# A fused recurrence and feed-forward kernel: w_in's first columns in two transfers, ScalarE copies two pairs' turned q, a new order table

## The chip, the cores and the metric

The kernel runs on one core of a Trainium2 chip. The metric is device time in microseconds (us). The engines of the core are TensorE (PE in the profile; PEld is its loading of weights), VectorE (DVE), ScalarE (ACT), GpSimd (POOL) and SyncE (SP). Each takes its instructions in program order. Loads, stores and the transposing transfers are issued by SP, the weights' transfers by POOL.

## The reference

Two stages in a row, all in float32. First a gated linear recurrence for 4 batches of 8 heads over 768 steps with heads of 48 elements, then a feed-forward layer (384 to 2048 to 384) with a leaky ReLU.

```python
f = 1.0 / (1.0 + np.exp(-f_logit))
for t in range(S):                                  # S = 768
    state = f[:, :, t, :, None] * state + np.einsum('bhd,bhe->bhde', k[:, :, t], v[:, :, t])
    y[:, :, t] = np.einsum('bhd,bhde->bhe', q[:, :, t], state)
x = y.transpose(0, 2, 1, 3).reshape(B * S, H * D)   # 3072 x 384
h = x @ w_in                                        # 384 x 2048
out = np.maximum(0.01 * h, h) @ w_out               # 2048 x 384
```

## The kernel before

The 768 steps are cut into 6 chunks of 128, and the 4 batches into 2 halves of two. A chunk with a half is a pair j (12 of them, j = 0 to 11), and each of its two batches is a unit a (0 or 1). A word such as `mx_0_1` in the order table means the part `mx` of pair 0, unit 1.

For a unit the work goes as follows. SP loads f, k, q and v (`Lf`, `Lk`, `Lq`, `Lv`, line 99). ACT forms the logarithm of the gate (`gate`, lines 135 and 136), PE sums it along the chunk with a triangle of ones and once more to the chunk's end (`cs`, lines 141 and 144), and ACT takes three exponentials of it (`dec`, lines 151, 152 and 155). DVE or POOL scales k and q by them (`k`, line 160; `q`, line 166), and POOL casts v (`v`, lines 173 and 174). PE turns k and q into PSUM (`tk`, `tq`, line 187), and DVE copies the turned tiles out (`ck`, `cq`, line 190); from pair 6 on a transposing transfer of SP does this instead (`xk`, `xq`, line 193). PE forms the scores (`sc`, line 206), DVE multiplies them by the triangle (`mk`, line 211), and PE mixes them with v, and with the state of the chunks before (`mx`, line 239). DVE copies the result out as the feed-forward input xT (`xt`, line 245). Beside that PE forms the chunk's own state (`pt`, line 250), DVE adds it (`sf`, lines 255 and 256) and POOL decays it (`sb`, lines 260 and 263).

The feed-forward layer takes w_in in groups. For pairs 0 to 3, whose units are done one by one, `uu_j_a_g` is group g of 4 blocks of 128 hidden columns (12 matmuls, line 290) and `pu` its leaky ReLU on ACT (line 295). Later pairs do both units at once (`up`, line 277; `pr`, line 283). `dn_j_a_q` is a quarter of the down-projection of a unit (4 matmuls, line 300); the last unit goes in two column parts (`dp`, line 322). DVE copies the result (`ob`, line 305) and SP stores it (`st`, line 313).

The weights come by POOL's transfers, which cast them from float32 to bfloat16: `W_0` to `W_2` bring the columns 0 to 511, 512 to 1023 and 1024 to 2047 of w_in (line 111), `W_3` to `W_6` the four quarters of w_out's rows (line 115). A one-element POOL copy (line 108) makes the first of them wait for v of pair 1, unit 0. `H_4` (line 127) is a small transfer on SP that waits for `W_4`; the loads of pair 2 stand behind it.

Nothing is scheduled by the compiler: `manual_schedule` keeps the order in which the words of the table (lines 348 to 403) are carried out, and each engine takes its own share of them in that order. PSUM tiles rotate: `ps_g` has 4 buffers for `cs`, `tp`, `pw`, `py` and `pt` (a score takes two), so each waits for the reader of the fourth one before it; `ps_m` has 2 for `uu` and `up`, `ps_o` 2 for `dn`. The loads rotate through 6 buffers of each kind.

Of the kernel before, what the change touches and what calls it, by code (L numbers as in the profile page):

```python
# [15 lines left out]
def kernel(  # L16
# [87 lines left out]
    def weights(piece, x, j, a):  # L104

        if (x, j, a) not in seen:
            seen.add((x, j, a))
            nc.gpsimd.tensor_copy(out=gate_w[:, 0:1], in_=raw(j, "fkqv"[x])[0:1, a, H - 1, D - 1:D])
        if piece < len(w_in_cols):
            lo, hi = w_in_cols[piece]  # L110
            nc.gpsimd.dma_start(out=w_in_b[piece], in_=moe_w_in[:, lo:hi].rearrange("(k p) n -> p k n", p=128))  # L111
        else:
            n = NF // 4
            part = piece - len(w_in_cols)
            nc.gpsimd.dma_start(  # L115
                out=w_out_b[:, part * n:(part + 1) * n, :],
                in_=moe_w_out[part * n * 128:(part + 1) * n * 128, :].rearrange("(p a) n -> p a n", a=n))
# [167 lines left out]
    def up_unit(j, a, g):  # L285
        pm = st[j]["pu", a, g] = ps_m.tile([128, 4, 128], FP32, name="pm", tag="pm")
        for i in range(4):
            ff = 4 * g + i
            for kk in range(NK):
                nc.tensor.matmul(pm[:, i, :], w_in(kk, ff), st[j]["xT"][:, kk, a, :],  # L290
                                 start=(kk == 0), stop=(kk == NK - 1))

# [66 lines left out]
    uu_1_1_3 dec_2_0 v_2_0 Lf_3_0 ob_0_0 dn_1_0_0 pu_1_1_2 dn_1_1_0 q_2_0 st_0_0 gate_2_1 dn_1_0_1 k_2_0 st_0_1 tq_2_0
    tk_2_0 cq_2_0 dn_1_1_1 Lk_3_0 ck_2_0 cs_2_1 sc_2_0 Lq_3_0 dec_2_1 v_2_1 pt_2_0 mk_2_0_0 dn_1_0_2 Lv_3_0 sb_0_1  # L360
    mk_2_0_1 dn_1_1_2 pu_1_1_3 q_2_1 gate_3_0 dn_1_0_3 Lf_3_1 sf_2_0 mx_2_0 Lk_3_1 dn_1_1_3 xt_2_0 tq_2_1 k_2_1 Lq_3_1
    uu_2_0_0 ob_1_0 cs_3_0 pu_2_0_0 Lv_3_1 uu_2_0_1 cq_2_1 dec_3_0 tk_2_1 v_3_0 uu_2_0_2 st_1_0 ck_2_1 pt_2_1 pu_2_0_1
    q_3_0 dn_2_0_0 Lf_4_0 sf_2_1 pu_2_0_2 uu_2_0_3 sb_1_1 k_3_0 Lk_4_0 sc_2_1 pu_2_0_3 tq_3_0 mk_2_1_0 Lq_4_0 dn_2_0_1
    gate_3_1 mk_2_1_1 tk_3_0 dn_2_0_2 Lv_4_0 v_3_1 cq_3_0 cs_3_1 ck_3_0 mx_2_1 Lf_4_1 dec_3_1 ob_1_1 sc_3_0 xt_2_1
    dn_2_0_3 st_1_1 k_3_1 q_3_1 pt_3_0 uu_2_1_0 mk_3_0_1 Lk_4_1 sb_2_0 tk_3_1 mk_3_0_0 pu_2_1_0 uu_2_1_1 Lq_4_1 sf_3_0
    dn_2_1_0 pu_2_1_1 Lv_4_1 mx_3_0 v_4_0 gate_4_0 pt_3_1 xt_3_0 tq_3_1 Lf_5_0 uu_2_1_2 gate_4_1 sf_3_1 dn_2_1_1
    Lk_5_0 ck_3_1 pu_2_1_2 uu_2_1_3 cq_3_1 ob_2_0 Lq_5_0 sc_3_1 pu_2_1_3 cs_4_0 mk_3_1_1 dn_2_1_2 dec_4_0 st_2_0
    mk_3_1_0 cs_4_1 dn_2_1_3 Lv_5_0 dec_4_1 k_4_0 q_4_0 mx_3_1 uu_3_0_0 Lf_5_1 v_4_1 gate_5_0 k_4_1 tk_4_0 Lk_5_1
    tq_4_0 xt_3_1 q_4_1 uu_3_0_1 pu_3_0_0 ck_4_0 tk_4_1 Lq_5_1 sb_2_1 cq_4_0 pu_3_0_1 cs_5_0 uu_3_0_2 ck_4_1 dec_5_0
    Lv_5_1 pt_4_0 sb_3_0 uu_3_1_0 sf_4_0 pu_3_0_2 Lf_6_0 tq_4_1 pt_4_1 k_5_0 dn_3_0_0 pu_3_1_0 v_5_0 sf_4_1 Lk_6_0  # L370
    gate_5_1 uu_3_1_1 sb_3_1 cq_4_1 dn_3_0_1 Lq_6_0 ob_2_1 pu_3_1_1 sc_4_2 q_5_0 uu_3_1_2 st_2_1 mk_4_0_0 dn_3_0_2
    mk_4_0_1 v_5_1 pu_3_1_2 Lv_6_0 tq_5_0 mk_4_1_0 uu_3_1_3 Lf_6_1 mk_4_1_1 tk_5_0 uu_3_0_3 Lk_6_1 ck_5_0 mx_4_2
    cq_5_0 pu_3_0_3 Lq_6_1 cs_5_1 xt_4_0 sb_4_0 dn_3_1_0 dec_5_1 Lv_6_1 xt_4_1 dn_3_0_3 sb_4_1 Lf_7_0 pu_3_1_3 pt_5_0
    dn_3_1_1 ob_3_0 sf_5_0 gate_6_0 up_4_0 st_3_0 q_5_1 k_5_1 dn_3_1_2 Lk_7_0 tq_5_1 dn_3_1_3 pr_4_0 cq_5_1 Lq_7_0
    cs_6_0 ob_3_1 tk_5_1 dec_6_0 up_4_1 Lv_7_0 ck_5_1 v_6_0 pt_5_1 cs_6_1 pr_4_1 sf_5_1 up_4_2 st_3_1 dec_6_1 dn_4_0_0
    Lf_7_1 up_4_3 pr_4_2 k_6_0 sc_5_2 Lk_7_1 pr_4_3 up_4_4 mk_5_0_0 Lq_7_1 dn_4_0_1 q_6_0 mk_5_1_0 pr_4_4 xk_6 pt_6_0
    mk_5_0_1 up_4_5 mk_5_1_1 pt_6_1 pr_4_5 up_4_6 xq_6 sf_6_0 mx_5_2 gate_7_0 sf_6_1 Lv_7_1 up_4_7 xt_5_0 sb_5_0
    dn_4_0_2 Lf_8_0 xt_5_1 pr_4_6 cs_7_0 pr_4_7 up_5_0 dec_7_0 Lk_8_0 cs_7_1 dn_4_0_3 pr_5_0 up_5_1 Lq_8_0 ob_4_0
    dec_7_1 dn_4_1_0 st_4_0 up_5_2 pr_5_1 q_7_0 sc_6_2 Lv_8_0 pr_5_2 dn_4_1_1 mk_6_0_0 Lf_8_1 up_5_3 sb_5_1 mk_6_1_1
    xq_7 dn_4_1_2 mk_6_1_0 pr_5_3 k_7_0 up_5_4 mk_6_0_1 Lk_8_1 dn_4_1_3 pr_5_4 Lq_8_1 mx_6_2 v_7_0 up_5_5 xt_6_0 xk_7  # L380
    sb_6_0 pt_7_0 xt_6_1 gate_8_0 dn_5_0_0 sf_7_0 up_6_0 Lv_8_1 sb_6_1 ob_4_1 dn_5_0_1 Lf_9_0 pr_5_5 cs_8_0 pr_6_0
    up_6_1 dec_8_0 cs_8_1 st_4_1 up_6_2 pr_6_1 dn_5_0_2 Lk_9_0 pr_6_2 pt_7_1 up_6_3 sf_7_1 Lq_9_0 dec_8_1 dn_6_0_0
    Lv_9_0 v_8_0 up_5_6 pr_6_3 sc_7_2 Lf_9_1 pr_5_6 k_8_0 up_6_4 mk_7_0_0 Lk_9_1 up_5_7 mk_7_1_0 pr_6_4 dn_6_0_1
    mk_7_0_1 Lq_9_1 q_8_0 pr_5_7 up_6_5 mk_7_1_1 xk_8 dn_5_0_3 pr_6_5 mx_7_2 ob_5_0 xq_8 dn_6_0_2 gate_9_0 xt_7_0
    sb_7_0 up_6_6 st_5_0 xt_7_1 pt_8_0 sb_7_1 up_7_0 sf_8_0 Lv_9_1 pr_6_6 pt_8_1 cs_9_0 pr_7_0 sf_8_1 up_7_1 dec_9_0
    Lf_10_0 up_6_7 cs_9_1 Lk_10_0 pr_7_1 dn_5_1_0 pr_6_7 up_7_2 Lq_10_0 dec_9_1 dn_6_0_3 Lv_10_0 up_7_3 pr_7_2 ob_6_0
    sc_8_2 v_9_0 Lf_10_1 pr_7_3 up_7_4 mk_8_1_1 st_6_0 dn_6_1_0 k_9_0 mk_8_0_1 pr_7_4 up_7_5 mk_8_0_0 Lk_10_1 dn_6_1_1
    mk_8_1_0 pr_7_5 q_9_0 xk_9 up_7_6 mx_8_2 pr_7_6 Lq_10_1 up_7_7 xq_9 xt_8_0 sb_8_0 dn_6_1_2 xt_8_1 pr_7_7 dn_5_1_1
    gate_10_0 Lv_10_1 dn_6_1_3 Lf_11_0 up_8_0 dn_5_1_2 pr_8_0 cs_10_0 Lk_11_0 up_8_1 dn_5_1_3 pr_8_1 Lq_11_0 cs_10_1
    dec_10_0 up_8_2 ob_5_1 Lv_11_0 pt_9_0 dn_8_0_0 dec_10_1 sf_9_0 st_5_1 up_8_3 ob_6_1 pr_8_2 k_10_0 sc_9_2 pr_8_3  # L390
    st_6_1 up_8_4 mk_9_0_0 dn_8_0_1 Lf_11_1 mk_9_1_0 sb_8_1 pr_8_4 up_8_5 xk_10 mk_9_1_1 pt_9_1 mk_9_0_1 dn_7_0_0
    pr_8_5 Lk_11_1 sf_9_1 up_8_6 Lq_11_1 mx_9_2 pr_8_6 dn_8_0_2 xt_9_0 sb_9_0 Lv_11_1 up_8_7 xt_9_1 dn_7_0_1 q_10_0
    pr_8_7 up_9_0 gate_11_0 dn_7_0_2 v_10_0 xq_10 dn_8_0_3 pr_9_0 dn_7_0_3 ob_8_0 sb_9_1 cs_11_0 up_9_1 st_8_0 ob_7_0
# [43 lines left out]
```

## Time and profile before

| what | us |
|---|---|
| median of 3 runs | 184.77 (184.28 to 184.93) |
| the profiled execution's own time | 185.62 |
| its span, first to last instruction | 183.9 |
| busy: PE, PEld, DVE, ACT, POOL | 169.2, 133.1, 90.0, 99.1, 75.2 |
| down-projection matmuls (line 300), 368 of them | 71.6 |
| up-projection matmuls (lines 277 and 290), 384 each | 51.5 and 27.5 |

Times in the trace count from the span's start. Busy time is the time in which at least one instruction of the engine ran; matmuls overlap, so a mean duration is longer than the distance from one to the next. The table of slices gives the busy share of each fortieth of the span (4.6 us) in tenths. The chain of waits is followed back from the last instruction: each row is a start, a length, an engine and a line, with the number of instructions merged. A DMA queue's row gives packets, megabytes and the time that the packets took as a share of 16 engines' time; q0 is POOL's queue, q1 is SP's.

### The profile page before, as it was taken

The numbers are of one execution on the slowest core, as the hardware profiler recorded it, in microseconds if no ns is written. First come the engines' busy times: TensorE is split into PE (matmuls) and PEld (weight loads), VectorE is DVE, ScalarE is ACT, GpSimd is POOL, SyncE is SP. The second block draws the span as 40 slices with busy tenths as digits, with TensorE's granted clock in tenths as the row PEclk, the third lists the DMA queues.
The fourth block names the chain that finished last, engine by engine and source line by source line (L and its number), as shares of the span: only waits on it lengthen the run. The fifth ranks groups of instructions, "written<-read, shape, count | busy, mean of one in ns | idle before, by whom it ended". The sixth has DMA issues, their size and how long they took to land.

```text
span 183.9 us, 5443 instructions
## 1 busy us (share of the span) xinstructions
PE 169.2 (92%) x2264; PEld 133.1 (72%) x2264; DVE 90.0 (49%) x188; ACT 99.1 (54%) x201; POOL 75.2 (41%) x138
## 2 busy tenths in 40 slices
PE   0467699999999999999999999999999999999993
...
GB/s 117 199 202 181 189 205 215 190 179 225 209 207 184 196 208 193 210 211 224 151 224 174 218 169 177 226 233 136 237 211 150 77 100 46 0 53 36 43 86 86
DMA packets 118208, 30.23 MB, mean 164 GB/s; under 512 B 113064, under 2 KB 117288, under 8 KB 118184
## 3 DMA queue, kind: packets, MB, share of 16 engines
...
## 4 chain that ended last, share of the span: by engine, by line
PE 87%; POOL 4%; SPq 3%; DMA 2%; issue 2%; DVE 0%; POOLq 0%
PE po L300 33%; PE pm L277 24%; PE pm L290 13%; PE py L239 5%; PE pw L206 4%; SPq L99 3%; DMA v_raw<-in_v_dram 2%; PE pt L250 2%; PE tp L187 2%; PE cs L141 2%; PE po L322 1%; POOL w_in_b L111 1%; POOL w_out_b L115 1%; PE cs L144 1%; POOL v_b L173 1%
## 5 line engine op out<-in xcount | busy, mean ns | idle before, releaser
L300 PE MATMUL po<-w_out_b,gT 128*128 128x384 bf16 x368 | 71.6, 326 | 0.0
L283 ACT ACTIVATE gT<-pm 128x512 bf16<-128x512 f32 x64 | 38.1, 599 | 32.5 <-PE pm L277 32.0
L277 PE MATMUL pm<-xT,w_in_b 128*128 128x256 bf16 x384 | 51.5, 273 | 0.0
L300 PEld LDWEIGHTS <-gT 128*128 128x128 bf16 x368 | 34.0, 98 | 15.8 <-issue 0.2
L277 PEld LDWEIGHTS <-w_in_b 128*128 128x128 bf16 x384 | 40.8, 114 | 5.3
L305 DVE COPY osb<-po 128x384 f32<-128x384 f32 x23 | 12.7, 555 | 47.4 <-PE po L300 47.2
L211 DVE TENSOR_TENSOR wm<-pw,ut 128x512 bf16<-128x512 f32 x48 | 30.2, 683 | 10.9 <-PE pw L206 10.7
L295 ACT ACTIVATE gT<-pm 128x512 bf16<-128x512 f32 x32 | 19.1, 600 | 22.7 <-PE pm L290 22.1
L290 PE MATMUL pm<-xT,w_in_b 128*128 128x128 bf16 x384 | 27.5, 226 | 0.0
L173 POOL CAST v_b<-v_raw 128x384 bf16<-128x384 f32 (+1 forms) x18 | 12.1, 672 | 35.5 <-DMA v_raw<-in_v_dram 25.1
L290 PEld LDWEIGHTS <-w_in_b 128*128 128x128 bf16 x384 | 24.7, 116 | 1.7 <-issue 0.2
L166 POOL TENSOR_TENSOR qh<-q_raw,a_t 128x384 bf16<-128x384 f32 (+1 forms) x12 | 15.7, 1309 | 14.6 <-ACT a_end L155 8.9
L245 DVE CAST xT<-py 128x384 bf16<-128x384 f32 x24 | 12.6, 552 | 12.0 <-PE py L239 11.8
L263 POOL CAST sb<-sf 64x192 bf16<-64x192 f32 x40 | 14.3, 357 | 9.5 <-PE py L239 7.3
L151 ACT ACTIVATE em_t<-cs 128x384 bf16<-128x384 f32 x24 | 11.8, 494 | 9.8 <-PE cs L144 8.9
L141 PE MATMUL cs<-lf,ut 128*128 128x384 bf16 x24 | 8.5, 352 | 6.9 <-ACT lf L136 6.1
L135 ACT ACTIVATE e_t<-f_raw 128x384 f32<-128x384 f32 (+1 forms) x18 | 11.4, 632 | 5.8 <-DMA f_raw<-in_f_logit_dram 5.8
L160 POOL TENSOR_TENSOR kh<-k_raw,em_t 128x768 bf16<-128x768 f32 x6 | 9.9, 1646 | 8.1 <-ACT em_t L151 8.0
L152 ACT ACTIVATE a_t<-cs 128x384 bf16<-128x384 f32 x24 | 11.9, 494 | 0.0
L136 ACT ACTIVATE lf<-e_t 128x384 bf16<-128x384 f32 (+1 forms) x18 | 11.4, 631 | 0.6
L255 DVE TENSOR_TENSOR sf<-sf,pt 64x192 f32<-64x192 f32 x20 | 6.9, 343 | 9.6 <-PE pt L250 4.3
L260 POOL TENSOR_TENSOR sf<-sf,a_end 128x192 f32<-128x192 f32 x20 | 10.6, 529 | 0.6 <-DVE sf L256 0.2
...
## 6 DMA issues: line engine op xcount, KB each, us to landing
...
```

The lines of the kernel that those rows point to most:

```text
L141: nc.tensor.matmul(t[:, 0:H * D], ut, lf[:, a, :, 0:D], start=True, stop=True)
L166: eng.tensor_mul(qhs[j % NR][:, a, :, 0:D], raw(j, "q")[:, a], st[j]["a"][:, a].rearrange("t a (h d) -> t a h d", d=D))
L173: nc.gpsimd.tensor_copy(out=vb[:, a], in_=raw(j, "v")[:, a])
L211: nc.vector.tensor_mul(wm, st[j].pop(("pw", a, i)), ut[:, None, :].to_broadcast([128, P2, 128]))
L245: nc.vector.tensor_copy(out=xT[:, :, a, :], in_=st[j].pop(("py", a))[:, 0:NK, :])
L263: nc.gpsimd.tensor_copy(out=sb[rows, a, :, i * D:i * D + D], in_=sf[rows, a])
L277: nc.tensor.matmul(pm[:, i, :], w_in(kk, ff), st[j]["xT"][:, kk].rearrange("t a s -> t (a s)"), start=(kk == 0), stop=(kk == NK - 1))
L283: nc.scalar.activation(gT[:, 2 * g:2 * g + 2, :], st[j].pop(("pm", g)), AF.Prelu, alpha=0.01)
L290: nc.tensor.matmul(pm[:, i, :], w_in(kk, ff), st[j]["xT"][:, kk, a, :], start=(kk == 0), stop=(kk == NK - 1))
L295: nc.scalar.activation(gT[:, 4 * g:4 * g + 4, 128 * a:128 * a + 128], st[j].pop(("pu", a, g)), AF.Prelu, alpha=0.01)
L300: nc.tensor.matmul(po, st[j]["g"][:, ff, 128 * a:128 * a + 128], w_out_b[:, ff, :], start=(ff == 0), stop=(ff == NF - 1))
L305: nc.vector.tensor_copy(out=osb, in_=st[j].pop(("po", a)))
```

## The change

The first 512 columns of w_in come as two transfers of 256 (`W_0`, `W_1`), so the other pieces' numbers go up by one, and the hold, `H_5`, waits for the same quarter of w_out as before. Hidden columns 0 to 511 are dealt to blocks in two sets of 256 instead of one of 512, and the rows of w_out's first quarter are laid out to match, in 256 rows of two instead of 128 of four. The first group of pair 0's two units is computed in halves of 6 matmuls (`uh`) with a leaky ReLU each (`ph`). For pairs 0 and 1 ACT copies the turned q. A transposing transfer may take one unit (no word of the table uses that). The whole order table is new; its beginning is shown, up to the first `cs_4_0`.

```diff
--- before.py
+++ after.py
@@ -40,6 +40,7 @@
     BY_UNIT = 6
     K_DVE = 6
     Q_DVE = 3
+    CQ_ACT = 2
 
     const = ctx.enter_context(tc.tile_pool(name="const", bufs=1))
     inp = ctx.enter_context(tc.tile_pool(name="inp", bufs=6))
@@ -74,7 +75,7 @@
     nc.gpsimd.memset(ones_col, 1.0)
     gate_w = const.tile([1, 8], FP32, tag="gate_w")
 
-    w_in_cols = ((0, FF // 4), (FF // 4, FF // 2), (FF // 2, FF))
+    w_in_cols = ((0, FF // 8), (FF // 8, FF // 4), (FF // 4, FF // 2), (FF // 2, FF))
     w_in_b = [const.tile([128, NK, hi - lo], BF16, name="w_in_b", tag=f"w_in{lo}") for lo, hi in w_in_cols]
     w_out_b = const.tile([128, NF, KD], BF16, tag="w_out")
 
@@ -112,9 +113,13 @@
         else:
             n = NF // 4
             part = piece - len(w_in_cols)
-            nc.gpsimd.dma_start(
-                out=w_out_b[:, part * n:(part + 1) * n, :],
-                in_=moe_w_out[part * n * 128:(part + 1) * n * 128, :].rearrange("(p a) n -> p a n", a=n))
+            rows = moe_w_out[part * n * 128:(part + 1) * n * 128, :]
+            if part == 0:
+                nc.gpsimd.dma_start(out=w_out_b[:, 0:n, :].rearrange("p (c a) n -> p c a n", c=2),
+                                    in_=rows.rearrange("(c p a) n -> p c a n", c=2, a=2))
+            else:
+                nc.gpsimd.dma_start(out=w_out_b[:, part * n:(part + 1) * n, :],
+                                    in_=rows.rearrange("(p a) n -> p a n", a=n))
 
     gate_s = const.tile([1, 32], BF16, tag="gate_s")
 
@@ -187,10 +192,18 @@
             nc.tensor.transpose(tp[:, p, :], scaled(j, x)[:, a, 2 * p:2 * p + 2, :], ident)
 
     def turn_out(j, a, x):
-        nc.vector.tensor_copy(out=turned(j, x)[:, P2 * a:P2 * a + P2, :], in_=st[j].pop(("tp" + x, a)))
-
-    def turn_dma(j, x):
-        nc.sync.dma_start_transpose(out=turned(j, x), in_=scaled(j, x).rearrange("t a h d -> t (a h d)"))
+        out, src = turned(j, x)[:, P2 * a:P2 * a + P2, :], st[j].pop(("tp" + x, a))
+        if x == "q" and j < CQ_ACT:
+            nc.scalar.copy(out=out, in_=src)
+        else:
+            nc.vector.tensor_copy(out=out, in_=src)
+
+    def turn_dma(j, x, a=None):
+        if a is None:
+            nc.sync.dma_start_transpose(out=turned(j, x), in_=scaled(j, x).rearrange("t a h d -> t (a h d)"))
+        else:
+            nc.sync.dma_start_transpose(out=turned(j, x)[:, P2 * a:P2 * a + P2, :],
+                                        in_=scaled(j, x)[:, a].rearrange("t h d -> t (h d)"))
 
     def units(a):
         return range(2) if a == 2 else (a,)
@@ -264,10 +277,13 @@
 
     def w_in(kk, ff):
 
-        c, a = divmod(ff, 4)
-        piece = [hi > 512 * c for lo, hi in w_in_cols].index(True)
-        lo = 512 * c - w_in_cols[piece][0]
-        return w_in_b[piece][:, kk, lo + a:lo + 512:4]
+
+        n = 2 if ff < 4 else 4
+        c, a = divmod(ff, n)
+        first = 128 * n * c
+        piece = [hi > first for lo, hi in w_in_cols].index(True)
+        lo = first - w_in_cols[piece][0]
+        return w_in_b[piece][:, kk, lo + a:lo + 128 * n:n]
 
     def up(j, g):
         pm = st[j]["pm", g] = ps_m.tile([128, 2, 256], FP32, name="pm", tag="pm")
@@ -290,6 +306,18 @@
                 nc.tensor.matmul(pm[:, i, :], w_in(kk, ff), st[j]["xT"][:, kk, a, :],
                                  start=(kk == 0), stop=(kk == NK - 1))
 
+    def up_half(j, a, h):
+        pm = st[j]["ph", a, h] = ps_m.tile([128, 4, 128], FP32, name="pm", tag="pm")
+        for i in range(2):
+            for kk in range(NK):
+                nc.tensor.matmul(pm[:, i, :], w_in(kk, 2 * h + i), st[j]["xT"][:, kk, a, :],
+                                 start=(kk == 0), stop=(kk == NK - 1))
+
+    def relu_half(j, a, h):
+        gT = once(j, "g", lambda: gpool.tile([128, NF, 256], BF16, name="gT", tag="gT"))
+        nc.scalar.activation(gT[:, 2 * h:2 * h + 2, 128 * a:128 * a + 128], st[j].pop(("ph", a, h))[:, 0:2, :],
+                             AF.Prelu, alpha=0.01)
+
     def relu_unit(j, a, g):
         gT = once(j, "g", lambda: gpool.tile([128, NF, 256], BF16, name="gT", tag="gT"))
         nc.scalar.activation(gT[:, 4 * g:4 * g + 4, 128 * a:128 * a + 128], st[j].pop(("pu", a, g)), AF.Prelu, alpha=0.01)
@@ -336,9 +364,9 @@
         "gate": gate, "cs": cs, "dec": dec, "k": scale_k, "q": scale_q, "v": cast_v,
         "tk": lambda j, a: turn(j, a, "k"), "tq": lambda j, a: turn(j, a, "q"),
         "ck": lambda j, a: turn_out(j, a, "k"), "cq": lambda j, a: turn_out(j, a, "q"),
-        "xk": lambda j: turn_dma(j, "k"), "xq": lambda j: turn_dma(j, "q"),
+        "xk": lambda j, a=None: turn_dma(j, "k", a), "xq": lambda j, a=None: turn_dma(j, "q", a),
         "sc": score, "mk": mask, "mx": mix, "xt": x_out, "pt": state, "sf": state_add, "sb": state_end,
-        "up": up, "pr": relu, "uu": up_unit, "pu": relu_unit, "W": weights, "H": hold, "dn": down, "ob": out_copy, "st": store,
+        "up": up, "pr": relu, "uu": up_unit, "uh": up_half, "ph": relu_half, "pu": relu_unit, "W": weights, "H": hold, "dn": down, "ob": out_copy, "st": store,
         "dp": down_part, "op": out_part, "sp": store_part,
         "Lf": lambda j, a: load(j, "f", a), "Lk": lambda j, a: load(j, "k", a),
         "Lq": lambda j, a: load(j, "q", a), "Lv": lambda j, a: load(j, "v", a),
@@ -346,60 +374,61 @@
...
     order = """
-    Lf_0_0 Lk_0_0 Lq_0_0 Lv_0_0 Lf_0_1 gate_0_0 Lk_0_1 Lq_0_1 cs_0_0 dec_0_0 Lv_0_1 v_0_0 Lf_1_0 k_0_0 q_0_0 tk_0_0
-    gate_0_1 Lk_1_0 tq_0_0 Lq_1_0 cs_0_1 cq_0_0 ck_0_0 pt_0_0 dec_0_1 Lv_1_0 sc_0_0 sf_0_0 v_0_1 Lf_1_1 mk_0_0_1
-    mk_0_0_0 gate_1_0 Lk_1_1 q_0_1 mx_0_0 Lq_1_1 k_0_1 cs_1_0 xt_0_0 tq_0_1 Lv_1_1 dec_1_0 tk_0_1 cq_0_1 W_0_3_1_0
-    pt_0_1 ck_0_1 k_1_0 sc_0_1 sb_0_0 gate_1_1 q_1_0 tk_1_0 sf_0_1 W_1_3_1_0 mk_0_1_0 cs_1_1 W_2_3_1_0 dec_1_1
-    mk_0_1_1 tq_1_0 W_3_3_1_0 ck_1_0 mx_0_1 W_4_3_1_0 k_1_1 W_5_3_1_0 cq_1_0 tk_1_1 W_6_3_1_0 q_1_1 v_1_0 xt_0_1
-    tq_1_1 ck_1_1 pt_1_0 v_1_1 cq_1_1 sc_1_0 sf_1_0 pt_1_1 uu_0_0_0 mk_1_0_0 mk_1_0_1 sc_1_1 pu_0_0_0 sf_1_1 mx_1_0
-    uu_0_1_0 sb_1_0 mk_1_1_1 uu_0_0_1 xt_1_0 pu_0_1_0 mk_1_1_0 pu_0_0_1 uu_0_1_1 mx_1_1 pu_0_1_1 uu_1_0_0 xt_1_1
-    uu_1_0_1 pu_1_0_0 uu_1_1_0 pu_1_0_1 uu_1_1_1 pu_1_1_0 pu_1_1_1 dn_0_1_0 uu_0_0_2 dn_0_0_0 pu_0_0_2 uu_0_0_3 H_4
-    Lf_2_0 Lk_2_0 uu_1_0_2 pu_0_0_3 Lq_2_0 dn_0_1_1 pu_1_0_2 uu_1_0_3 dn_0_0_1 pu_1_0_3 uu_0_1_2 Lv_2_0 dn_0_0_2
...
+    Lf_0_0 Lk_0_0 Lq_0_0 Lv_0_0 Lf_0_1 gate_0_0 Lk_0_1 Lq_0_1 cs_0_0 dec_0_0 Lv_0_1 v_0_0 Lf_1_0 q_0_0 k_0_0 tq_0_0
+    gate_0_1 Lk_1_0 tk_0_0 Lq_1_0 cq_0_0 cs_0_1 ck_0_0 pt_0_0 dec_0_1 Lv_1_0 sc_0_0 sf_0_0 v_0_1 Lf_1_1 q_0_1 mk_0_0_1
+    tq_0_1 gate_1_0 Lk_1_1 mk_0_0_0 Lq_1_1 cq_0_1 cs_1_0 k_0_1 mx_0_0 dec_1_0 Lv_1_1 tk_0_1 xt_0_0 W_0_3_1_0 pt_0_1
+    q_1_0 W_1_3_1_0 ck_0_1 gate_1_1 sf_0_1 sc_0_1 W_2_3_1_0 cs_1_1 mk_0_1_1 W_3_3_1_0 k_1_0 dec_1_1 v_1_0 mk_0_1_0
+    tk_1_0 W_4_3_1_0 tq_1_0 ck_1_0 sb_0_0 k_1_1 mx_0_1 cq_1_0 q_1_1 tk_1_1 W_5_3_1_0 xt_0_1 sc_1_0 v_1_1 ck_1_1 tq_1_1
+    mk_1_0_0 uh_0_0_0 cq_1_1 W_6_3_1_0 uh_0_1_0 mk_1_0_1 ph_0_0_0 sc_1_1 W_7_3_1_0 ph_0_1_0 pt_1_0 mk_1_1_0 mx_1_0
+    uh_0_0_1 xt_1_0 uh_0_1_1 ph_0_0_1 sf_1_0 pt_1_1 ph_0_1_1 uu_0_1_1 mk_1_1_1 uu_1_0_0 pu_0_1_1 mx_1_1 pu_1_0_0
+    uu_1_0_1 xt_1_1 uu_1_1_0 pu_1_0_1 uu_1_1_1 pu_1_1_0 uu_0_0_1 pu_1_1_1 uu_0_0_2 pu_0_0_1 uu_1_1_2 pu_0_0_2 dn_0_0_0
+    pu_1_1_2 uu_1_0_2 uu_0_0_3 pu_1_0_2 H_5 Lf_2_0 dn_1_0_0 pu_0_0_3 Lk_2_0 uu_1_1_3 Lq_2_0 dn_1_0_1 pu_1_1_3 dn_0_0_1
+    uu_1_0_3 dn_1_0_2 pu_1_0_3 Lv_2_0 dn_0_0_2 Lf_2_1 uu_0_1_2 dn_0_0_3 gate_2_0 Lk_2_1 dn_1_0_3 ob_0_0 Lq_2_1 cs_2_0
+    ob_1_0 dn_0_1_0 dec_2_0 sf_1_1 uu_0_1_3 st_0_0 pu_0_1_2 dn_0_1_1 q_2_0 v_2_0 st_1_0 pu_0_1_3 k_2_0 tq_2_0 dn_0_1_2
+    sb_0_1 gate_2_1 cq_2_0 Lv_2_1 tk_2_0 dn_1_1_0 ck_2_0 Lf_3_0 sc_2_0 cs_2_1 Lk_3_0 mk_2_0_0 dn_1_1_1 dec_2_1
+    mk_2_0_1 Lq_3_0 dn_0_1_3 mx_2_0 q_2_1 Lv_3_0 dn_1_1_2 xt_2_0 v_2_1 pt_2_0 k_2_1 Lf_3_1 uu_2_0_0 ob_0_1 sb_1_0
+    tk_2_1 gate_3_0 Lk_3_1 tq_2_1 sf_2_0 cq_2_1 pu_2_0_0 cs_3_0 st_0_1 sb_1_1 ck_2_1 uu_2_0_1 dec_3_0 dn_2_0_0 Lq_3_1
+    sb_2_0 pu_2_0_1 sc_2_1 uu_2_0_2 Lv_3_1 mk_2_1_1 q_3_0 dn_2_0_1 Lf_4_0 mk_2_1_0 pu_2_0_2 uu_2_0_3 v_3_0 k_3_0
+    gate_3_1 Lk_4_0 tq_3_0 pt_2_1 dn_1_1_3 cq_3_0 pu_2_0_3 Lq_4_0 sf_2_1 tk_3_0 cs_3_1 dn_2_0_2 ck_3_0 Lv_4_0 dec_3_1
+    ob_1_1 mx_2_1 v_3_1 sc_3_0 st_1_1 xt_2_1 dn_2_0_3 q_3_1 k_3_1 gate_4_0 Lf_4_1 uu_2_1_0 mk_3_0_1 tq_3_1 pu_2_1_0
+    tk_3_1 Lk_4_1 mk_3_0_0 uu_2_1_1 cq_3_1 Lq_4_1 cs_4_0 ck_3_1 mx_3_0 dec_4_0 sc_3_1 Lv_4_1 v_4_0 xt_3_0 dn_2_1_0
...
```

Beyond that the table has the same words, except that pair 10's second unit, and not pair 11's, is the one that is computed last and in two column parts.

More of the change, by code (lines that the diff above doesn't have):

```diff
@@ L359 @@
[L359 to L393, printed above, removed]
@@ new lines @@
+    uu_3_1_1 sf_4_1 tq_4_1 Lq_5_1 pu_3_1_1 uu_3_1_2 cq_4_1 dn_3_0_1 ck_4_1 Lv_5_1 pu_3_1_2 sc_4_2 Lf_6_0 uu_3_1_3
+    mk_4_1_0 uu_2_1_2 mk_4_0_1 Lk_6_0 pu_3_1_3 dn_3_0_2 mk_4_0_0 pu_2_1_2 Lq_6_0 uu_3_0_3 mk_4_1_1 gate_5_1 pt_3_1
+    Lv_6_0 cs_5_0 sf_3_1 mx_4_2 dec_5_0 Lf_6_1 cs_5_1 pu_3_0_3 uu_2_1_3 k_5_0 q_5_0 Lk_6_1 dn_2_1_2 xt_4_0 pu_2_1_3
+    v_5_0 xt_4_1 tk_5_0 Lq_6_1 dec_5_1 dn_3_0_3 sb_3_1 dn_2_1_3 Lv_6_1 k_5_1 up_4_0 v_5_1 ob_2_1 Lf_7_0 pt_5_0 tq_5_0
+    q_5_1 sf_5_0 dn_3_1_0 gate_6_0 st_2_1 up_4_1 ck_5_0 tk_5_1 Lk_7_0 dn_3_1_1 ck_5_1 pr_4_1 cq_5_0 tq_5_1 dn_3_1_2
```

42 lines of the change are left out of this document (32 added, 10 removed).

## The prediction

> **What bounds the kernel now.** I read the busy table and its slices first, then the stages (busy time of each engine between two instants), then the chain of waits around the place where TensorE becomes dense, then the DMA view in one-microsecond windows.
>
> ```profile
> PE 169.2 (92%) x2264; PEld 133.1 (72%) x2264; DVE 90.0 (49%) x188; ACT 99.1 (54%) x201; POOL 75.2 (41%) x138
> PE   0467699999999999999999999999999999999993
> ```
>
> TensorE (PE) is idle for 183.9 - 169.2 = 14.7 us, in the first five slices and the last alone. The stages say it more exactly (length, then each engine's busy time and instructions):
>
> ```profile
> 20.00:22.00 2.00, 0.76 (x12) 0.49 (x11) 0.64 (x3) 0.00 (x0) 1.65 (x5) 1.00 1.14 176
> 22.00:24.00 2.00, 1.96 (x24) 1.71 (x19) 1.96 (x5) 0.00 (x0) 1.68 (x5) 1.00 1.15 207
> 40.00:60.00 20.00, 20.00 (x293) 15.17 (x291) 14.45 (x30) 11.04 (x27) 8.83 (x18) 1.00 0.93 198
> 60.00:100.00 40.00, 40.00 (x663) 32.09 (x662) 26.58 (x55) 27.96 (x61) 24.51 (x42) 1.00 1.03 200
> 100.00:140.00 40.00, 40.00 (x519) 32.08 (x518) 18.11 (x37) 25.98 (x51) 21.18 (x33) 1.00 1.03 199
> 140.00:181.00 41.00, 41.00 (x436) 31.56 (x434) 12.45 (x22) 16.01 (x29) 5.29 (x7) 1.00 0.23 63
> ```
>
> From 22 us to 181 us PE has no hole; the last 2.85 us are the copy and store of the last tile. So the end is: the instant at which PE becomes dense, plus the work then left, plus a tail that the change does not shorten. How it becomes dense, in the chain (start, length, what):
>
> ```profile
> 18.58 2.18 POOL w_out_b L115 x4
> 20.81 0.51 POOL v_b L173
> 21.36 0.48 PE pt L250 x4
> 21.84 0.54 PE pw L206 x8
> 22.42 0.48 PE pt L250 x4
> 22.90 1.28 PE pm L290 x12
> 25.26 2.98 PE pm L290 x36
> 30.06 1.50 PE pm L290 x24
> ```
>
> PE resumes at 21.36, when GpSimd (POOL), done with issuing seven weight transfers, casts v of pair 1 (`v_1_0`). A matmul of line 290 takes 1.28/12 = 107 ns at first and 1.50/24 = 62 ns later: PE runs at half speed until 27.0 (13 matmuls of line 290 start from 26 to 27 us, 20 from 27 to 28), 5.6 us after 21.36.
>
> **The weights' arrival.** The first w_in transfer (512 columns, 384 KB) is issued at 14.64 and lands 7.0 us later, at 21.6; the next land at 23.8 and 27.5, the four of w_out at 29.5, 31.2, 33.7 and 35.2. Their packets, read in one-microsecond windows (packets, MB, time as a share of 16 engines; the windows 20 to 21, then 24 to 25, then 27 to 28):
>
> ```profile
> q0 software_dynamic: 161, 0.16, 106.1%
> ...
> q0 software_dynamic: 98, 0.20, 109.8%
> ...
> q0 software_dynamic: 80, 0.22, 110.3%
> ```
>
> A packet is one row of the tile. 1 KB takes 16 x 1.061 us / 161 = 105 ns, 2 KB 179 ns, 3 KB 221 ns.
>
> **Part 1, w_in's first transfer in two.** Same 384 rows each, of 512 B. No row shows such a packet: above it stands 105 ns (1 KB), below it about 15 ns (192 B loads; 1,187 of them take 114% of the window from 15 to 16). The line through 1 and 2 KB (74 ns per KB) gives 68 ns; I take that, as the nearest rows are on it. 24 rows per engine: 24 x 68 = 1.6 us instead of 2.5, so columns 0 to 255 land 0.9 to 1.4 us before 21.6: at 20.2 to 20.7. (The first packets come at about 17.4; the last engine ended 4 us later because it still served v's load; the low end scales the 4 us by 68/105.) Both pieces take 3.3 us, so all later pieces land 0.7 us later. The first quarter of w_out now has 256 rows of 1.5 KB (16 per engine, 142 ns: 2.3 us) for 128 of 3 KB (8 x 221: 1.8 us): 0.5 more, 1.2 in all behind it. Two DMAs issued in a row do not wait for each other (the w_out pieces land 1.5 to 2.5 us apart, the time of their bytes). The Trainium skill, "DMA: Bandwidth & Descriptors", Anatomy of one DMA, gives each such DMA a fixed cost of about 2 us; paid in series the second DMA would add 2.0 us and not 0.7, which overruns a margin of 0.7 found below by 0.6 and gives 183.9. These landings do not show it in series.
>
> POOL issues one transfer more (0.77 to 0.95 us each by line 111), but `v_1_0` now stands ahead of the w_out issues and `sb_0_0` behind them: 14.64 + 4 x 0.85 = 18.0, `v_1_0` done at 18.9 instead of 21.6. So the wait that starts the chain above goes; what is late next is the weight itself and DVE.
>
> **Part 2, q's turned tile copied by ScalarE (ACT).** Four copies of 128x512 leave DVE (0.41 to 0.42 us each by line 190). On ACT no row shows them: 0.41 us (DVE's) below, 0.60 us (line 295, same shape out of PSUM) above; I take 0.60, the same engine. ACT idles 6.0 us before its first line-295 instruction (24.21), which covers them. `cq_0_0` waits behind `gate_0_1` until 8.85 and ends at 9.45; `sc_0_0` started at 9.74 anyway. Without that cover each would delay its scores by up to 0.6.
>
> **Part 3, the halves.** Two groups of 12 matmuls become four of 6, and two ACT instructions of 0.60 become four of about 0.39 (between 0.19 for 4 columns and 0.49 for 384): 0.4 us more ACT, where it waits 22 us on PE in all. PE's work is the same.
>
> **When PE becomes dense afterwards.** I walk DVE's new order with start-to-start times of the trace (k or q 0.47, mask 0.60, kT copy 0.34, state add 0.75, xT 0.47): `q_0_1` 10.67, two masks, `k_0_1` 12.35, `xt_0_0` 13.7 (after `cs_1_0`, 12.73, and `mx_0_0`), `q_1_0` 14.2 (its decay ends then), `ck_0_1`, `sf_0_1`, `mk_0_1_1` 15.8 (scores at 15.15), `k_1_0`, `mk_0_1_0`, `ck_1_0` 17.7, `k_1_1`, `q_1_1`, `xt_0_1` 19.0 to 19.5. `tq_1_1` must wait for that (its PSUM slot is `mx_0_1`'s), and `uh_0_0_0` follows at 20.1; with full durations instead, 20.65. The weights allow 20.2 to 20.7. I take 20.4. Before, the same work would have started at 21.36 + 0.58 = 21.94 (`sc_1_0`, 0.58 with its step, is now done earlier). **Gain 21.94 - 20.4 = 1.5 us**, if PE's speed-up comes at the same distance (5.1 us: at 25.5 instead of 27.0).
>
> **What follows must keep up.** In the new order PE reaches `uu_0_1_1` (columns 512 to 1023, landing 24.5) at 25.1, `uu_0_0_2` (28.2) at about 30.0, `dn_0_0_0` (w_out, 30.7) at about 31.4. The hold moves from 31.2 to 32.4, and with it unit 2's loads. `f_2_1` landed at 41.0, now 42.3, and its gate must begin by 42.7 so that `cs_2_1` (45.28, now 43.8) does not wait; pair 3's first gate must begin by 47.2 (`cs_3_0` 50.23, less 1.5, less one down-projection quarter of 0.65 that moves behind it, plus a transpose of 0.22, less 1.1 of gate) and its load lands at 44.3 + 1.2 = 45.5; pair 4's by the same count at 57.1 against 55.4. So margins of 0.4 to 0.7 us, no stall; I add none. Tail and steady state have the same matmuls.
>
> **Sum.** The profiled execution: span 183.9, time 185.62 (1.72 around it), which is 0.85 above the median 184.77. 183.9 - 1.5 = 182.4, with 1.72 184.1, less 0.85: **183.3 us**, 0.8% faster. Its own range is 182.9 to 184.2 (start 20.0 to 21.0, or 0.3 of new small waits).
>
> **Rivals.**
> 1. *PE speeds up earlier.* The forecast counts the 5.1 us from 20.4. In the new order PE has few holes from `tk_1_1` at 18.7 on; counted from there it is 23.8, and 1.7 us of half-speed work takes half: 0.8 more, **182.5**. Against: before, the stretch from 12 to 20 us had stages of over 80% busy and did not speed it up. The Trainium skill, "TensorE: Matmul & The Clock Gate", What's actually happening, says that the clock opens after a whole free-running window of some 3.4 us is busy, and Part 4 that transposes do not count. The 5.6 us agree; from 20.4 that gives 23.8 to 27.2.
> 2. *The start is not won.* The 512 B rows land no sooner (21.6: one engine still serves v's load), or the speed-up stays at 27.0: 0.3 gained, **184.5**, not to be told from no change. For it: the last engine set the landing before.
> 3. *Slower: a row costs the same whatever its length.* Then the split adds 2.5 us to the weight stream and w_out's first quarter 1.8. PE starts at 21.6, stands at `dn_0_0_0` (in order, all behind it waits) from 32.6 to 33.8, which is 1.2, and the hold, 4.3 later, makes `f_2_1` land at 45.3 and `cs_2_1` wait 0.3; 0.3 of start is kept: 184.77 + 1.2 + 0.3 - 0.3 = **186.0**. It decides as soon as the stream lengthens by more than about 2 us. Against: 105, 179 and 221 ns grow with the row. The other order of the remaining work would show in the same way, as holes of PE between 31 and 65 us, where before there were none.
>
> **Chances.** Forecast 0.42, rival 1 0.16, rival 2 0.20, rival 3 0.22. A run tells about 0.3% (0.55 us): faster 0.58, same 0.20, slower 0.22. The range, 182.3 to 186.0, leaves out half of rival 3 and some of rival 1.
>
> **What would show it.** First w_in landing at or before 20.7; the first matmul of the halves at 20.1 to 20.7 rather than 22.7; `v_b` of pair 1 cast near 18; 56 ns matmuls from about 25.5; PE 100% busy in every stage from 26 us. It is wrong if PE shows idle time after 26 us, if the first half waits for xT or q rather than w_in until after 21.5, or if the copies on ACT delay the exponentials of pair 1.

## The result and the profile after

The changed kernel takes 182.96 us (median of 17 runs, 182.06 to 184.39) against 184.93 (17 runs beside it, 183.87 to 185.91): ratio 0.9908, interval 0.9885 to 0.9932, so 1.3 to 2.1 us less (1.7 by the ratio, 2.0 by the medians). The forecast was 183.3 us, 1.5 us less. The profiled execution took 183.06 us with a span of 181.3, which is 2.6 us under the profiled one of before; part of that is the chance of single runs, as shown below.

The busy table, and the stages (length, busy time and instructions of PE, PEld, DVE, ACT, POOL, then clock, DMA share, GB/s) of the changed kernel:

```profile
PE 168.4 (93%) x2264; PEld 131.4 (72%) x2264; DVE 88.1 (49%) x184; ACT 101.3 (56%) x207; POOL 76.3 (42%) x139
```

```profile
18.00:20.00 2.00, 1.96 (x33) 1.30 (x33) 2.00 (x6) 0.59 (x1) 1.85 (x5) 1.00 1.30 174
20.00:22.00 2.00, 2.00 (x23) 1.65 (x21) 1.07 (x2) 1.35 (x3) 1.95 (x5) 1.00 1.21 197
...
40.00:60.00 20.00, 20.00 (x324) 15.02 (x323) 15.84 (x34) 13.11 (x33) 11.61 (x24) 1.00 0.99 212
60.00:100.00 40.00, 40.00 (x631) 32.52 (x630) 24.43 (x52) 26.68 (x57) 21.85 (x38) 1.00 1.01 201
```

PE's work is the same and has no hole from 18.6 us on (before: from 21.4). The clock column reads 1.00 in the first rows although PE still runs at half speed there: the trace's first record of the granted clock is its rise at 23.5 us, so ahead of that the distance of the matmuls has to be read. The chain shows how the dense stretch starts:

```profile
11.29 3.98 DMA f_raw<-in_f_logit_dram
...
16.43 0.48 PE cs L146
16.90 0.08 PE cs L149 x4
16.99 1.03 PE tp L192 x8
18.01 0.59 PE py L252 x15
18.60 0.00 issue
18.60 0.61 PE tp L192 x4
19.21 0.54 PE pw L219 x8
19.75 0.54 PE tp L192 x4
20.29 1.28 PE pm L313 x12
21.57 0.54 PE pw L219 x8
22.11 0.43 PE pt L263 x4
22.54 0.55 PE py L252 x14
23.09 0.99 PE pm L313 x12
24.25 1.47 PE pm L306 x24
```

Line 313 is the halves. The first of their matmuls starts at 20.08 (before, the first w_in matmul: 22.70), and the distance of matmuls falls from 107 to 56 ns at 23.5 (before: 27.0). In this profile PE hardly waits from 16.4 us on, and the chain goes back to the load of f for pair 1, unit 1, which landed at 15.3. DVE is no more than level with PE: xT of pair 0, unit 1, ended at 19.48, and `tq_1_1`, which waits for it, began at 19.68, straight behind the scores (line 219). In the second profile of the same kernel `tq_1_1` follows xT at once, and the chain goes through DVE:

```profile
18.67 0.48 DVE xT L258
19.15 0.04 issue
19.19 0.59 PE tp L192 x4
19.78 1.28 PE pm L313 x12
```

POOL's own order in the first profile, over the same time:

```profile
14.11 3.27 POOL L112 DMA_DIRECT2D w_in_b<-in_moe_w_in_dram  x4
17.38 0.52 POOL L178 CAST v_b<-v_raw 128x384 bf16<-128x384 f32 x1
...
18.06 0.74 POOL L118 DMA_DIRECT2D w_out_b<-in_moe_w_out_dram  x1
```

v of pair 1 is cast at 17.4 (before 20.8), between the w_in issues and those of w_out. The first w_in transfer lands 4.3 us after its issue, at 18.4, and the later ones at 20.5, 23.5 and 26.6; w_out's quarters at 28.5, 31.3, 32.5 and 34.4.

**The 2.6 us of the two profiles.** The same work began at 21.94 before and begins at 20.08: 1.86. The half-speed stretch behind that point lasted 5.1 us and lasts 3.4; half of the difference is 0.84. The sum is 2.7. Behind that, 2052 matmuls are left at 28.51 before and at 25.98 now, the same number from each part of the program, and PE takes 152.5 us for them in both: the new order of the rest makes no difference. The 1.86 is counted from a late start of before: its chain leads through v of pair 1, which landed at 14.5 us there, and in the eleven other profiles with that release of the weights at 13.4 to 14.1. So 1.86 need not be the usual gain of the start. With one profile of that kernel, and starts at 20.08 and 19.57 in the two of the changed one, the usual gain is not shown.

### The profile page after: what moved, and what is told of

It reads as the page before. It is cut to its first block, busy times and chain, and to the rows that moved or that the text cites. A ratio compares the mean times of both kernels' runs of the same rounds, so it can differ in the third digit from the quotient of the medians.

```text
span 181.3 us, 5431 instructions
## 1 busy us (share of the span) xinstructions
PE 168.4 (93%) x2264; PEld 131.4 (72%) x2264; DVE 88.1 (49%) x184; ACT 101.3 (56%) x207; POOL 76.3 (42%) x139
## 4 chain that ended last, share of the span: by engine, by line
PE 89%; SPq 6%; DMA 2%; ACT 1%; issue 0%; DVE 0%
PE po L328 34%; PE pm L293 24%; PE pm L306 12%; PE py L252 6%; SPq L100 6%; PE pw L219 4%; PE tp L192 3%; PE cs L146 2%; DMA f_raw<-in_f_logit_dram 2%; PE pt L263 2%; PE po L350 1%; PE pm L313 1%; PE cs L149 1%; ACT e_t L140 0%; ACT lf L141 0%
## 5 line engine op out<-in xcount | busy, mean ns | idle before, releaser
L299 ACT ACTIVATE gT<-pm 128x512 bf16<-128x512 f32 x64 | 37.8, 599 | 32.7 <-PE pm L293 32.3
L293 PEld LDWEIGHTS <-w_in_b 128*128 128x128 bf16 x384 | 40.0, 110 | 6.3
L224 DVE TENSOR_TENSOR wm<-pw,ut 128x512 bf16<-128x512 f32 x48 | 30.5, 684 | 17.6 <-PE pw L219 17.4
L178 POOL CAST v_b<-v_raw 128x384 bf16<-128x384 f32 (+1 forms) x18 | 11.1, 617 | 41.2 <-DMA v_raw<-in_v_dram 31.9
L323 ACT ACTIVATE gT<-pm 128x512 bf16<-128x512 f32 x30 | 17.9, 598 | 12.7 <-PE pm L306 11.9
L306 PE MATMUL pm<-xT,w_in_b 128*128 128x128 bf16 x360 | 24.2, 219 | 0.0
L306 PEld LDWEIGHTS <-w_in_b 128*128 128x128 bf16 x360 | 21.9, 110 | 1.7
L258 DVE CAST xT<-py 128x384 bf16<-128x384 f32 x24 | 12.7, 554 | 16.8 <-PE py L252 16.7
L165 POOL TENSOR_TENSOR kh<-k_raw,em_t 128x768 bf16<-128x768 f32 x6 | 9.9, 1648 | 10.8 <-ACT em_t L156 7.4
L149 PEld LDWEIGHTS <-lf 128*128 128x128 bf16 x80 | 5.2, 100 | 7.6 <-issue 6.2
```

What stands on the lines that cost most here:

```text
L224: nc.vector.tensor_mul(wm, st[j].pop(("pw", a, i)), ut[:, None, :].to_broadcast([128, P2, 128]))
L258: nc.vector.tensor_copy(out=xT[:, :, a, :], in_=st[j].pop(("py", a))[:, 0:NK, :])
L299: nc.scalar.activation(gT[:, 2 * g:2 * g + 2, :], st[j].pop(("pm", g)), AF.Prelu, alpha=0.01)
L323: nc.scalar.activation(gT[:, 4 * g:4 * g + 4, 128 * a:128 * a + 128], st[j].pop(("pu", a, g)), AF.Prelu, alpha=0.01)
```

## The experiments

The theory on record: TensorE's dense work starts earlier since the new order takes the wait for pair 1's v off its path; the start is then set by DVE's xT (theory 1). Rivals: the split of the weights, or ACT's copies, made the gain; theory 2 is about the clock. Each ratio is to the kernel before, run beside it. The last column is the first record of a full granted clock; four traces have none (changed, again; copies on DVE; the last two of the kernel before), and there it is the matmul from which on the distance is 56 ns.

| run | ratio | interval | first w_in landing | first w_in matmul | clock open from |
|---|---|---|---|---|---|
| changed | 0.9908 | 0.9885 to 0.9932 | 18.4 | 20.08 | 23.5 |
| changed, again | 0.9857 | 0.9823 to 0.9890 | 19.3 | 19.57 | 22.5 |
| copies on DVE | 0.9895 | 0.9858 to 0.9932 | 19.7 | 19.75 | 22.7 |
| one transfer | 0.9932 | 0.9899 to 0.9965 | 19.6 | 19.68 | 23.2 |
| one transfer, again | 0.9931 | 0.9901 to 0.9961 | 20.2 | 20.27 | 24.0 |
| one transfer, whole group | 0.9938 | 0.9901 to 0.9974 | 21.4 | 21.46 | 25.0 |
| earlier release | 0.9913 | 0.9877 to 0.9949 | 18.0 | 19.87 | 24.8 |
| before, three words moved | 0.9927 | 0.9899 to 0.9954 | 19.8 | 19.81 | 23.9 |
| before, split alone | 1.0047 | 1.0016 to 1.0077 | 19.6 | 22.68 | 25.1 |
| before, words moved and split | 1.0001 | 0.9974 to 1.0029 | 18.7 | 19.94 | 23.9 |
| 30 added matmuls | 0.9872 | 0.9831 to 0.9913 | 18.9 | 19.44 | 10.8, again 24.5 |
| 90 added matmuls | 0.9880 | 0.9839 to 0.9921 | 20.2 | 20.19 | 12.0 |
| 90 added, earlier release | 0.9847 | 0.9812 to 0.9881 | 18.5 | 20.68 | 13.5 |

**The changed kernel with one transfer** (and the pieces renumbered), twice:

```diff
-    w_in_cols = ((0, FF // 8), (FF // 8, FF // 4), (FF // 4, FF // 2), (FF // 2, FF))
+    w_in_cols = ((0, FF // 4), (FF // 4, FF // 2), (FF // 2, FF))
```

> The changed kernel, but w_in's first 512 columns come in one transfer again (everything else as changed: halves, ScalarE copies, order). In the changed kernel's trace the first transfer landed at 18.4 us and was used at 20.1, when VectorE had made xT of pair 0, unit 1. Theory 1 (the start of the dense work is set by VectorE's chain, the split is worth little): one transfer of 1 KB rows lands at about 19.5 to 20.0, the halves start at 20.0 to 20.4, and the time stays 1.4 to 2.0 us under the kernel before. Rival (the split makes the gain): the transfer lands at 21 us or later, the start moves with it, and at most 0.8 us of the gain is left.

> The changed kernel with w_in's first 512 columns in one transfer, once more. Three kernels with one transfer gave 0.9927 to 0.9938 of the kernel before, three with two gave 0.9857 to 0.9908. If the split is worth something with the new order (the landing of one transfer varied between 19.6 and 21.4 us, and the start was 0.05 us after it in all three profiles): 0.9 to 1.5 us under the kernel before, and the first w_in matmul within 0.1 us of the landing where that is after 19.6. Rival (the split is worth nothing): 1.7 to 2.3 us under it.

Both times are 1.3 us under the kernel before. That lies between the two expectations of the first run, and the second expected just that. The chain of the second run shows the landing as the start:

```profile
13.63 6.60 DMA w_in_b<-in_moe_w_in_dram
...
20.27 1.46 PE pm L313 x12
```

Behind one transfer the start waits for the weight in all three profiles (0.05 us after the landing), which varies from 19.6 to 21.4. So theory 1 holds for the changed kernel, whose weight was there 1.7 and 0.3 us early in its two profiles, and is too strong in "the split is worth little".

**One transfer and whole groups:**

```diff
...
-    mk_1_0_0 uh_0_0_0 cq_1_1 W_6_3_1_0 uh_0_1_0 mk_1_0_1 ph_0_0_0 sc_1_1 W_7_3_1_0 ph_0_1_0 pt_1_0 mk_1_1_0 mx_1_0
-    uh_0_0_1 xt_1_0 uh_0_1_1 ph_0_0_1 sf_1_0 pt_1_1 ph_0_1_1 uu_0_1_1 mk_1_1_1 uu_1_0_0 pu_0_1_1 mx_1_1 pu_1_0_0
...
+    mk_1_0_0 uu_0_0_0 cq_1_1 W_5_3_1_0 mk_1_0_1 pu_0_0_0 sc_1_1 W_6_3_1_0 pt_1_0 mk_1_1_0 mx_1_0
+    uu_0_1_0 xt_1_0 pu_0_1_0 sf_1_0 pt_1_1 uu_0_1_1 mk_1_1_1 uu_1_0_0 pu_0_1_1 mx_1_1 pu_1_0_0
...
```

> The changed kernel with w_in's first 512 columns in one transfer and pair 0's first group whole (12 matmuls and one leaky ReLU for each unit), the new order else, ScalarE's copies kept. Theory 1: the same matmuls in the same place, start at 20.0 to 20.4, time 1.4 to 2.0 us under the kernel before. Rival (the halves let TensorE go on while the second transfer and the masks come): 0.5 us or more is lost against the changed kernel, as holes of TensorE between 20 and 25 us.

Neither came: the start is at 21.46, where the weight lands, and the time is 1.15 us under the kernel before. It runs as the kernel above it, and PE has no hole behind its start: whole or half groups make no difference that shows beside one transfer.

**ScalarE's copies undone** (`CQ_ACT = 0`):

> The changed kernel, but VectorE copies the turned q of pairs 0 and 1 again. Theory 1: two or three of the four copies stand on VectorE ahead of xT of pair 0, unit 1 (0.34 to 0.41 us each), so that xT comes 0.7 to 1.2 us later, the halves start at 20.8 to 21.3, and the time is 0.5 to 1.0 us under the kernel before. Rival (the copies are off the path): no change, 1.4 to 2.0 us under it.

The rival is right: the copies are worth nothing that shows. The chain:

```profile
17.97 0.41 DVE qT L199
18.38 0.47 DVE qh L171
18.84 0.48 DVE xT L258
...
19.37 0.58 PE tp L192 x4
19.95 1.28 PE pm L313 x12
```

One copy is now on DVE's path, and xT still comes at 18.8 (changed kernel: 18.9, with the copies on ACT at 0.58 us each). DVE has waits for PE ahead of it that take up the copies: 2.7 us between 8 and 19.5 us in the changed kernel, 1.4 us here. The two profiles alone would not settle it, since the load of f from which both chains come landed 0.6 us earlier here; the times do.

**The kernel before with three words moved:**

```diff
-    tq_1_1 ck_1_1 pt_1_0 v_1_1 cq_1_1 sc_1_0 sf_1_0 pt_1_1 uu_0_0_0 mk_1_0_0 mk_1_0_1 sc_1_1 pu_0_0_0 sf_1_1 mx_1_0
+    tq_1_1 ck_1_1 v_1_1 cq_1_1 sc_1_0 uu_0_0_0 pt_1_0 pt_1_1 mk_1_0_0 mk_1_0_1 sc_1_1 pu_0_0_0 sf_1_0 sf_1_1 mx_1_0
```

> The kernel before with three words moved: pt_1_0 and pt_1_1 behind uu_0_0_0, and sf_1_0 behind the masks of pair 1, unit 0. TensorE no longer waits for pair 1's v before the first w_in matmuls. Theory 1 (the weight's landing at 21.6 us is then what is late): first w_in matmul at 21.5 to 21.8 instead of 22.7 with two state products still to do, 0.1 to 0.6 us under the kernel before. Rival (the wait for v on GpSimd's queue was the whole cause): 1.2 us or more under it.

The gain is 1.35 us (0.9 to 1.9 by the interval), over twice the most that theory 1 expected and in the range of the rival: the wait for v was worth as much as all of the new order with one transfer. The landing at 21.6, on which the expectation was built, was that of the late run told of above; here the weight landed at 19.8, and the first w_in matmul followed at 19.81.

**The split alone, in the order of before:**

> The kernel before with w_in's first 512 columns in two transfers issued one behind the other, and w_out's first quarter laid out to match; its order, whole groups and VectorE's copies stay. Theory 1 (without the new order the split only adds an issue ahead of pair 1's v on GpSimd): v of pair 1 is cast at 21.6 instead of 20.8 us, the first w_in matmul comes at 23.2 to 23.6 instead of 22.7, and the time is 0.3 to 1.0 us above the kernel before. Rival (the split itself makes the gain): the time is 0.5 us or more under it.

The time is as theory 1 expected, 0.9 us slower. The instants are not: v was cast at 20.9 and the first w_in matmul came at 22.68, as in the profile of before, since v itself landed 0.8 us earlier than there. PE's waits (total, times, longest) show where it stood:

```profile
PE pt L254 <- POOL v_b L177: 1.8, 1, 1.8
```

The two pieces had landed at 19.6 and 20.7, and PE stood until 21.4 for v, whose cast is queued behind one more issue (7.1 us after the weights' release instead of 6.3). Only part of the loss is seen, though: the median span of these runs is 183.5 us against 183.1 beside it, 0.4 longer, where the median times differ by 1.1 (185.89 and 184.82). The rest lies outside the span, and its cause stays open.

**Both: three words moved, split and half groups of unit 0:**

> The kernel before with the three words moved (state products of pair 1 behind the first w_in matmuls), and w_in's first 512 columns in two transfers with unit 0's first group in halves; VectorE's copies and the rest of the order stay as before. Theory 1 (the order opens the start, and the split then takes the weight's landing off it): the first w_in matmul at 19.6 to 20.9, time 1.4 to 2.2 us under the kernel before, against 1.3 without the split. Rival (the split is worth nothing there either): 1.0 to 1.4 us under it.

Neither: all the gain is gone, though the start came at 19.9. The chain behind it ends at w_out's first quarter:

```profile
18.34 11.14 DMA w_out_b<-in_moe_w_out_dram
...
29.52 0.81 PE po L319 x4
```

This order reaches the down-projection earlier than the new one, and the split makes the stream longer. But the wait there was 0.2 us in the profile, which was the fastest of the kernel's runs (183.8, median 184.7); where the other runs lost 0.9 us more stays open.

**The changed kernel again, and with an earlier release** (`W_0_2_1_0` for `W_0_3_1_0`, and so on):

> The changed kernel once more, unedited, beside the others on one chip. Theory 1 and 2: 1.3 to 2.2 us under the kernel before; in the profile the first w_in matmul at 19.6 to 20.6 us whatever the first transfer's landing up to then, and the clock opening between 3.4 and 6.8 us after it or after the matmuls just before it, at another point than 23.5 us since the grid has no fixed place. Rival (the clock opens at a fixed distance of the first w_in matmul): 3.3 to 3.5 us after it again.

> The changed kernel with the weights' transfers released by q of pair 1, unit 0, instead of its v, without added matmuls. Theory 1 (the start is VectorE's xT, and the cold clock covers the weight stream behind it): the transfers land 0.4 to 0.9 us earlier, the first w_in matmul stays at 19.6 to 20.3, and the time stays 1.5 to 2.3 us under the kernel before. Rival (the landing sets the start): 0.4 to 0.9 us more.

The first came out better than expected (2.6 us under the kernel before, by the interval 2.0 to 3.3; the two measurements of the changed kernel meet at 0.9885 to 0.9890). The second is in time (1.6 us) and start as theory 1 has it: the weight landed at 18.0, and the start at 19.87 was DVE's. But behind DVE stands a load, of q for pair 1, unit 1:

```profile
12.42 5.90 DMA q_raw<-in_q_dram
...
18.41 0.56 DVE qh L171
18.97 0.48 DVE xT L258
```

It landed at 18.3, in the changed kernel at 16.7 and 16.2; the two runs with the earlier release have it latest of all profiles (18.3 and 17.9). That the earlier weights hold it up is likely, but not shown. The speed-up came 2.9 us and 4.9 us after the first w_in matmul, so not at a fixed distance.

**Matmuls added in TensorE's idle places,** 30, then 90, then 90 with the earlier release:

```diff
+    def dummy(n):
+        t = ps_o.tile([128, KD], FP32, name="po", tag="po")
+        for _ in range(n):
+            nc.tensor.matmul(t[:, 0:128], ident, ut, start=True, stop=True)
...
```

> The changed kernel with 30 added matmuls (128 columns, identity by triangle, into a PSUM tile that nobody reads) in TensorE's idle places between 7 and 16.5 us; nothing is left out. In the changed kernel's trace the spacing of matmuls fell from 107 to 56 ns at 23.4 us, 3.3 us after the first matmul of w_in. Theory 2 (the speed-up follows a stretch of unbroken matmuls): the spacing falls by 17 to 20 us, the dense work from 20 to 23.4 us takes half as long, and the time is 1.2 to 2.4 us under the changed kernel's, 3 to 4 us under the kernel before. Rival (it follows the w_in matmuls alone, or a time of its own): the spacing falls at 23 us or later, and the time is that of the changed kernel or up to 0.5 us above it.

> The changed kernel with 90 added matmuls (identity by triangle, 128 columns, into a PSUM tile that nobody reads) in every idle place of TensorE from 7.5 us to the first w_in matmul; nothing is left out. In the run with 30 of them the clock opened at 10.8 us, closed again at 17.6 and opened at 24.5, on a grid of 3.41 us, after windows in which TensorE was idle in part. Theory 2 (a window counts when it is full of matmuls): the clock opens by 12 us and stays open, the matmuls of w_in are 56 ns apart from the first on, the time is 1.0 to 2.5 us under the changed kernel's, and the runs spread less (under 1.5 us, where the changed kernel's 17 runs spread over 2.3 us), since the moment of opening no longer moves the dense work. Rival (the added matmuls delay the chain that makes xT and q as much as the open clock gives): the time is that of the changed kernel within 0.6 us.

> The changed kernel with the 90 added matmuls of the run before, and with the weights' transfers released by q of pair 1, unit 0, instead of its v, which lands 0.5 to 0.9 us later; nothing is left out. With the clock open early TensorE stood 0.93 us before uu_0_1_1 until the third w_in transfer landed at 23.65. Theory 3 (with the clock open the weight stream is the bound): the stream comes 0.4 to 0.9 us earlier, uu_0_1_1 with it, and the time is 2.3 to 3.2 us under the kernel before. Rival (the weights take from pair 1's loads what they gain, and the start moves back): 1.3 to 2.2 us under it, as the changed kernel.

With 30 the clock opened at 10.8 us and closed again, so neither expectation came whole: the dense work from 20 us was at half speed until 24.5, as the rival has it. The column behind the engines is the granted clock:

```profile
14.00:17.60 3.60, 2.19 (x42) 1.54 (x42) 3.56 (x9) 2.52 (x6) 3.60 (x6) 1.00 1.29 197
17.60:21.00 3.40, 3.05 (x32) 2.46 (x34) 2.85 (x6) 1.06 (x4) 3.21 (x7) 0.51 1.16 155
21.00:24.40 3.40, 3.40 (x49) 2.86 (x46) 2.54 (x5) 1.11 (x3) 1.43 (x4) 0.50 1.14 212
24.40:26.00 1.60, 1.60 (x39) 1.39 (x38) 0.01 (x1) 0.86 (x2) 0.00 (x0) 0.98 1.14 207
```

A stretch in which PE was busy 2.2 of 3.6 us cost it. With 90 it stayed open from 12 us, and the time was still that of the changed kernel: the rival was right in the time, but not in the cause it named, since xT of pair 0, unit 1, began at 18.8, no later than in the changed kernel. PE's waits in that run from 19 us on:

```profile
PE pm L306 <- DMA w_in_b<-in_moe_w_in_dram: 0.8, 1, 0.8
PE tp L192 <- POOL qh L171: 0.5, 1, 0.5
```

At full speed PE reaches columns 512 to 1023 before they land (23.65): the cold clock had hidden the weight stream. The second wait, at 51.2 us for a q that POOL scales, does not occur in the changed kernel. Of the 1.7 us that an open clock should give (half of 3.4), the two take 1.3; the rest is not followed. With the earlier release both waits are gone, though the start moved to 20.68 with xT (19.5). The time is 2.8 us under the kernel before, as theory 3 expected, and the ratio, 0.9847, is the lowest measured. Its interval lies just under that of the changed kernel's 17 runs and overlaps that of its second five, so it isn't shown to be faster. The spread was 1.5 and 1.4 us, as expected, but over five runs each (the changed kernel's second five spread over 1.0), so it tells nothing.

## Why the prediction was right

**The start: right, and by its step.** Predicted were xT of pair 0, unit 1 at 19.0 to 19.5 and the halves at 20.1 to 20.7; they came at 18.94 and 20.08, within 0.1 us of the ranges, and the chain runs through `tq_1_1` as said, though PE's own queue was as late as xT in that profile. The 1.5 us for it measured 1.86 from profile to profile.

**The weights: the packet right, the queue wrong.** A row of 512 B takes about 70 ns (predicted 68): from 19 to 19.5 us, 164 packets took 143.8% of 16 engines. But packets flowed already between 16 and 17 us, where before there were none:

```profile
q0 software_dynamic: 193, 0.10, 82.2%
```

So the first piece landed 1.8 us before the lower end predicted, and the rest of the stream 1.0 to 2.2 us earlier than the forecast said. The mis-sized term is the time from issue to first packet, taken as 2.8 us from one run (its trace has the first packet 2.5 us after the issue) and here 1.7; another 0.5 is the issue itself, at 14.11 instead of 14.64, since v landed earlier. The margins behind the start were thus wider than thought, and no wait came, as forecast. One row length was misread: the 221 ns for 3 KB divide by 80 packets, of which the same view counts nine of under 512 B, and without them it is 249 ns:

```profile
DMA packets 80, 0.22 MB, mean 216 GB/s; under 512 B 9, under 2 KB 9, under 8 KB 80
```

The 1.5 KB rows, put at 142 ns, took 135. The new layout of w_out's first quarter so lengthens the stream by about 0.2 us and not 0.5, which changes neither the sum nor a stall.

**The copies: sized right (0.58 for 0.60), off the path.** The prediction walked DVE's new order without them and left it open what they cost there; the run with them on DVE says: nothing that shows.

**The clock: wrong by 2 us, nearer to rival 1.** The forecast took 5.1 us from start to speed-up, so 25.5; it came at 23.5, where rival 1 had 23.8. Seven profiles of the new order without added matmuls show 2.9 to 4.9 us from the first w_in matmul, mean 3.6. That is worth some 0.7 us against the profile of before. Rival 1's reason, that the count begins at the dense work from 18.7 on, isn't shown: the distance is another in each run.

**The number: luck in part.** From profile to profile the time fell by 2.56 us and not by 1.5, 1.06 more (0.36 in the start, up to 0.84 in the clock). Against that, the forecast took off 0.85 us, by which the profiled run of before lay above its median; the profiled run of the changed kernel lies only 0.10 above its own, so 0.75 too much was taken off. The two errors leave the 0.3 us between 183.3 and 182.96. A late start and a late speed-up in the one profile of before would account for both; a second profile of it, which could show that, is not on record.

**The shares.** Of the gain, 1.15 to 1.35 us come without the split (the new order with one transfer, or the three words alone). The split adds on average: the four measurements of the new order with two transfers and no added matmuls lie at 0.9857 to 0.9913, the three with one at 0.9931 to 0.9938, some 0.4% or 0.7 us; the intervals of three of the four overlap with theirs, so this share is likely rather than shown. It needs the whole new order: alone the split costs 0.9 us, and beside the three words it takes all of their gain, for a reason that stays open. Rival 3 (rows cost the same whatever their length) is refuted by the 70 ns, rival 2's "lands no sooner" by the landings. Rival 2 also put one price, 0.3 us gained, on two cases; a start at 20.4 with the speed-up kept at 27.0 would have gained about 0.8 (half of 1.5).
